# Fused attention and two MLPs on one core: the first weight's low halves and the early turned tiles formed by TensorE in PSUM, the second weight's norm from a Gram diagonal, and a new order

## The chip, the cores and the metric

One core of a Trainium2 chip. The metric is device microseconds of one execution; a stated time is the median of several runs. The engines are TensorE (PE, with its weight loads as PEld), VectorE (DVE), ScalarE (ACT), GpSimd (POOL) and SyncE (SP), which issues the DMAs.

## The reference

Three steps follow one another, on 2304 tokens:

```python
scores = scale * q @ k.T + alibi_bias          # 4 x 8 heads, 576 rows, D = 64, window of 128
x = softmax(scores) @ v                        # -> (2304, 512)
h = x @ w_in                                   # 512 x 1024
solu = h * softmax(h)
ln = (solu - mean) / sqrt(var + 1e-6) * g_ln
x = ln @ w_out                                 # 1024 x 512
h2 = x @ w2_in                                 # 512 x 2048
out = (h2 * sigmoid(h2)) @ w2_out              # 2048 x 512
```

q, k, v and the gain are float32. The four weights arrive as 64-bit floats, and the kernel turns them into 32-bit ones on the chip.

## The kernel before

The 2304 rows are 18 blocks of 128 (`i`), and 9 chunks of two blocks (`c`). Every product of the MLPs and of attention with V is made of float16 halves: a number is a high half plus a low half, and `high*high + high*low + low*high` are three float16 matmuls.

**Weights.** There are 48 pieces of 128x512 ("slots" 0 to 47 of the tile `W`): 8 of w_in, 8 of w_out, 16 of w2_in, 16 of w2_out. A piece is loaded into `stage` as pairs of 32-bit words (512 KB). `decode` makes float32 of it: ACT shifts the high words (L456), DVE scales the low words (L458) and puts both together (L460, result in `W`). From the decoded pieces a norm is taken, which gives a power of two as the weight's scale: as a rule by `gram`, a matmul of a tile with itself (L396), whose diagonal DVE sums (`trace`, L407) or takes the maximum of (`column_max`, L401). For w_out, ACT squares each piece with the gain as scale (L508) and a matmul with ones adds the squares up (L513). Then `split_weight` makes the halves. A table `E_W` says how for each slot: "G" scales the piece (L347 on ACT, L348 on DVE or L350 on POOL), copies it to float16 (L342 on ACT, L343 on DVE) and subtracts (L354 on DVE or L355 on POOL); "V" scales straight to the high half and makes the low half in one DVE instruction (L533).

**Blocks.** For each block `a_qk` makes scores in PSUM (`sa`, L688), `a_max` adds the bias and takes the row maximum on DVE (L714), and ACT takes exponentials (L719, tile `e`). `a_parts` splits the result into halves (tile `a`) and turns it by a DMA transpose on SP's queue (L746, tile `aT`). `a_av` multiplies with V (L773), `a_evac` scales (L786, `xm`), `x_turn` splits and turns again (`xT`). A table `ON_PE` has "D" for a DMA transpose, and "P" for a turn on TensorE: `turned_parts` transposes float32 128x128 tiles into PSUM (L566), ACT copies the high half out (L568), and DVE subtracts it from the PSUM tile (L569). "P" stands for `xT` of blocks 1 to 3 and for `lnT` of block 1. Then come the first product (`m1_in`, L820), the softmax gate and norm (`layer_norm`, L834 to L870), the turn to `lnT`, and for each chunk the second product (`m1_out`, L920), whose result is split into `y` (L925 on ACT, L928 on DVE). For each chunk `m2_in` (L957) makes eight tiles of h2, ACT and DVE form the gate (L966 to L970), and `m2_out` (L984) accumulates the result; ACT evacuates it (L990), SP stores it.

**Order.** All of this is recorded first. A list scheduler (`Sched`) then places the instructions, with hand-set costs and with priorities from the tables `RANK`, `SLOPE` and `LATER`; the emitted program is a fixed order on each engine. Engines run in that order and wait on semaphores. `PICK` fixes for each split which engine does it. `JOINT` says whether two head pairs of a block share one PSUM area, `ROOT` and `NORM` which engine makes the inverse root and the normalisation, `V_AT` at which block a batch's norm of V is placed. The PSUM tag `mm` has two buffers, which turned tiles, products and norms take in turn.

Of the kernel before, what the change touches and what calls it, by code (L numbers as in the profile page):

```python
# [298 lines left out]
def fused_kernel(ctx, tc, qk, qn, kn, vt, rel, w_in, w_out, g_ln, w2_in, w2_out, out):  # L299
# [89 lines left out]


# [82 lines left out]
    def load_weight(name, w, slot0, n, cols, gain=None, columns=False):
# [4 lines left out]
        for at in range(0, n, 2):  # L478
# [12 lines left out]
            def go(at, k, sl):  # L491
                if gain is None:
                    size = n // nf if columns else n
                    if at % size == 0:
                        sums[name] = Buf(ps_early, [P, 512], F32, "gram", 2)

                    def high(x):
                        w = W.tile.rearrange("p s c -> p (s c)").bitcast(BF16).rearrange("p (s c h) -> p s c h", h=2, c=512)
                        return w[:, sl, x * P:(x + 1) * P, 1]
                    gram(sums[name], 4, high, [(W, sl)], 4 * (at % size), 4 * size - 1, columns)  # L500
                    if at % size == size - 1:
                        if columns:
                            column_max(sums[name], acc, at // size)
                        else:
                            trace(sums[name], acc)
                    return
                sq = Buf(early, [P, 512], BF16, "sq", 2)
                act(512, lambda: A.activation(sq.tile, W[:, sl, :], AF.Square, scale=gain[:, k:k + 1]),  # L508
                    [(W, sl), gain], [sq], extra=1)
                if at == 0:  # L510
                    sums[name] = Buf(ps_early, [P, 512], F32, "gram", 2)
                c = sums[name]
                pe(216, lambda: T.matmul(c.tile, ones.tile, sq.tile, start=at == 0, stop=at == n - 1), [ones, sq], [c])  # L513
                if at == n - 1:
                    v(512, lambda: V.tensor_reduce(acc.tile, c.tile, AX.X, ALU.add), [c], [acc])
# [14 lines left out]

# [698 lines left out]
```

## Time and profile before

| | |
|---|---|
| time, median of 3 runs | 731.42 us (730.77 to 731.5) |
| profiled execution, its own time | 729.44 us |
| its span in the trace | 727.5 us |
| mean granted clock of TensorE | 0.981 |
| busy: PE, DVE, ACT, POOL | 93%, 61%, 48%, 19% of the span |

The span is the time from the first to the last instruction of the profiled execution; 1.94 us lie around it. The busy shares are means over the whole program, which has a first part in which weights are decoded and the first blocks run, and a long second part of matmuls.

### The profile page before, as it was taken

The page shows a single profiled execution, that of the slowest core. Times are in us where ns is not written, and L with a number is a line of the kernel's source. Part 1 is how long each engine was busy: PE and PEld are TensorE (multiplying, and loading weights), DVE is VectorE, ACT ScalarE, POOL GpSimd, SP SyncE. Part 2 cuts the span into 40 slices and gives each one's busy share as a digit, 9 for nine tenths or more (in the row PEclk, how much of TensorE's full clock was granted, in tenths as well). Part 3 has the DMA queues.
Part 4 walks back from the last instruction along what each step waited for, and adds up shares of the span by engine and source line. Part 5 has one row for each costly group of instructions (what it writes and reads, how often), then busy time and mean ns, then how long its engine had stood idle before and what let it go on. Part 6 is the DMA issues. An engine that isn't in the chain of part 4 may idle for free.

```text
span 727.5 us, 13956 instructions
## 1 busy us (share of the span) xinstructions
PE 674.3 (93%) x5541; PEld 464.0 (64%) x5541; DVE 444.8 (61%) x1125; ACT 346.2 (48%) x738; POOL 138.5 (19%) x140
## 2 busy tenths in 40 slices
PE   4563688999999999999999999999999999999997
PEld 2432367778565577667766676678566777657853
DVE  3899999996897747553556657547672523321220
ACT  5687668575646635444454445525341422231231
POOL 1223034322443312130322112101010200100000
PEclk9996799999999999999999999999999999999999
DMA  9999985593535534251723454334250421100000
GB/s 309 346 247 273 241 199 134 131 231 89 99 78 103 130 73 81 53 114 31 145 59 73 82 107 90 91 56 73 44 102 1 68 65 30 30 30 1 1 30 29
DMA packets 142209, 75.82 MB, mean 104 GB/s; under 512 B 126656, under 2 KB 126784, under 8 KB 142144
## 3 DMA queue, kind: packets, MB, share of 16 engines
q1 hardware_dynamic: 142144, 74.94, 44.2%
q8 instruction: 43, 0.70, 0.4%
q14 instruction: 22, 0.18, 0.1%
HBM read 39.52 MB, written 4.72 MB: 61 GB/s over the span
## 4 chain that ended last, share of the span: by engine, by line
PE 79%; DVE 14%; ACT 3%; issue 2%; DMA 1%; POOL 0%; DVEq 0%; POOLq 0%; ACTq 0%
PE mm L984 25%; PE mm L957 23%; PE mm L920 12%; PE mm L820 11%; PE sa L688 4%; DVE W L460 3%; PE mm L773 2%; DVE stage L458 2%; DVE e L714 1%; PE gram L396 1%; DVE W L533 1%; PE sa L773 1%; DVE W L354 1%; DMA aT<-a 1%; DVE W L348 1%
## 5 line engine op out<-in xcount | busy, mean ns | idle before, releaser
L957 PE MATMUL mm<-y,W 128*128 128x256 f16 x1728 | 210.4, 273 | 1.1 <-DVE t L967 0.7
L984 PE MATMUL mm<-W,g 128*128 128x512 f16 x864 | 204.9, 379 | 0.0
L957 PEld LDWEIGHTS <-W 128*128 128x128 f16 x1728 | 167.0, 98 | 39.8 <-issue 2.0
L984 PEld LDWEIGHTS <-g 128*128 128x128 f16 x864 | 81.8, 98 | 78.7 <-issue 0.2
L820 PE MATMUL mm<-W,xT 128*128 128x512 f16 x432 | 105.2, 390 | 1.7 <-DVE xT L569 1.0
L920 PE MATMUL mm<-lnT,W 128*128 128x256 f16 x864 | 104.8, 273 | 0.0
L920 PEld LDWEIGHTS <-W 128*128 128x128 f16 x864 | 84.0, 98 | 19.7 <-issue 0.5
L719 ACT ACTIVATE e<-e,mx 128x256 f32<-128x256 f32 (+1 forms) x144 | 70.0, 487 | 45.9 <-DVE mx L714 43.3
L970 DVE SCALAR_TENSOR_TENSOR g<-t,g 128x512 f16<-128x512 f32 x72 | 55.5, 774 | 53.7 <-ACT g L969 53.3
L355 POOL TENSOR_TENSOR a<-e,a 128x512 f16<-128x512 f32 (+1 forms) x45 | 54.9, 1222 | 143.2 <-ACT a L342 65.8
L969 ACT ACTIVATE g<-t 128x512 f16<-128x512 f32 x72 | 45.0, 626 | 72.6 <-PE mm L984 61.1
L967 DVE SCALAR_TENSOR_TENSOR t<-t,mm 128x512 f32<-128x512 f32 x72 | 48.7, 682 | 48.3 <-ACT t L966 48.3
L966 ACT ACTIVATE t<-mm,cs 128x512 f32<-128x512 f32 x72 | 48.1, 680 | 62.5 <-PE mm L957 58.6
L820 PEld LDWEIGHTS <-xT 128*128 128x128 f16 x432 | 42.7, 100 | 47.6 <-issue 4.6
L688 PE MATMUL sa<-k,q 64*128 64x128 f32 x544 | 49.4, 312 | 17.1 <-DVE mx L714 12.2
L714 DVE CUSTOM_DVE_ANT_0 e<-sa,table 128x256 f32<-128x256 f32 (+1 forms) x144 | 53.9, 400 | 11.3 <-PE sa L688 6.3
L688 PEld LDWEIGHTS sa<-k,q 64*128 64x128 f32 x544 | 38.5, 202 | 29.1 <-DVE mx L714 15.7
L928 DVE SCALAR_TENSOR_TENSOR y<-mm,cs,y 128x512 f16<-128x512 f32 x18 | 13.3, 748 | 57.1 <-ACT y L925 57.1
L834 DVE TENSOR_REDUCE lnst<-mm 128x1 f32<-128x1024 f32 x18 | 22.0, 1220 | 42.0 <-PE mm L820 42.0
L848 POOL TENSOR_SCALAR lnst<-lnst 128x1 f32<-128x1 f32 x17 | 3.5, 203 | 214.0 <-ACT mm L845 214.0
L925 ACT ACTIVATE y<-mm,cs 128x512 f16<-128x512 f32 x18 | 12.2, 686 | 64.0 <-PE mm L920 56.3
L773 PEld LDWEIGHTS <-aT 128*128 128x128 f16 x816 | 32.9, 101 | 15.2 <-issue 8.6
(151 smaller groups left out, 707.9 us busy)
## 6 DMA issues: line engine op xcount, KB each, us to landing
stage<-in_moe_w_in_dram SPq DMA_DIRECT2D x24, 512.0 KB, 5.3
stage<-in_moe_w_out_dram SPq DMA_DIRECT2D x24, 512.0 KB, 4.5
k<-in_kn_dram SPq DMA_DIRECT2D x18, 256.0 KB, 2.9
q<-in_qn_dram SPq DMA_DIRECT2D x18, 256.0 KB, 3.1
vraw<-in_vt_dram SPq DMA_DIRECT2D x18, 256.0 KB, 3.8
out_dram<-t SPq DMA_DIRECT2D x18, 256.0 KB, 2.3
aT<-a SPq DMA_TRANSPOSE x72, 3.3
lnT<-ln SPq DMA_TRANSPOSE x34, 3.2
```

Of the source, the lines that this page charges most:

```text
L355: ("G", cg(n), lambda: G.tensor_tensor(dst(), a(), b(), op), True)], r, w, pick=pick)
L688: T.matmul(SA[:, j, off + sl * P:off + (sl + 1) * P], q[rows, p, :], k[rows, p, :], start=True, stop=sl not in blank)
L714: v(n + 20, lambda j=j: V.tensor_tensor_reduce(e[:, j, lo:lo + n], SA[:, j, off + lo:off + lo + n], table[:, 2 * p + j, o:o + n], -0.125, ...
L719: act(n, lambda j=j: A.activation(e[:, j, lo:lo + n], e[:, j, lo:lo + n], AF.Exp, bias=mx[:, j:j + 1], scale=-1.0, accum_out=rs[:, 2 * p + ...
L773: T.matmul(heads(i)[:, h // 4, h % 4, :], t[:, (2 * ha + j) * nh + c, :], vb[sl][:, h, hv, :], start=(n == 0), stop=(n == 3 * nh - 1))
L820: T.matmul(pt[:, half * 512:(half + 1) * 512], x[:, hx, k, :], W16(2 * k + half, hw), start=(k == 0 and hx + hw == 0), stop=(k == KD - 1 a ...
L920: T.matmul(pt[:, ct % 2], W16(8 + k, hw)[:, ct * P:(ct + 1) * P], l[:, hx * KF1 + k, :], start=(k == 0 and hw + hx == 0), stop=(k == KF1 - ...
L957: T.matmul(pt[:, mm], W16(16 + 4 * k + m // 4, hw)[:, (m % 4) * P:(m % 4 + 1) * P], y[:, hx, k, :], start=(k == 0 and hw + hx == 0), stop= ...
L966: act(512, lambda: A.activation(t.tile, flat(pt.tile), AF.Tanh, scale=cs[:, 0:1]), [pt, (cs, 0)], [t], extra=1)
L967: v(512, lambda: V.scalar_tensor_tensor(out=t.tile, in0=t.tile, scalar=1.0, in1=flat(pt.tile), op0=ALU.add, op1=ALU.mult), [t, pt], [t])
L970: v(512, lambda: V.scalar_tensor_tensor(out=flat(g[:, 1]), in0=t.tile, scalar=2.0 ** -16, in1=flat(g[:, 0]), op0=ALU.mult, op1=ALU.subtrac ...
L984: T.matmul(pt.tile, g[:, hg, mm, b * P:(b + 1) * P], W16(32 + m, hw), start=(m == 0 and hg + hw == 0), stop=(m == KF2 - 1 and hg == 1))
```

## The change

Five things change.

1. `E_W` is "P" for the eight slots of w_in. The high half is scaled straight from the decoded piece (as in "V"). The low half is formed in PSUM: a float32 matmul of the piece with a diagonal matrix that holds the scale (`diag`), then a float16 matmul of the high half with minus the identity (`minus`), accumulated onto it; ACT or DVE copies the result out (DVE for slots 0 to 5, ACT for 6 and 7).
2. `ON_PE` has "Q" for `aT` and `xT` of blocks 0 to 3 and for `lnT` of blocks 0 and 1: turned on TensorE, high half copied out by ACT, minus the high half accumulated in PSUM, and the low half copied out by ACT too. The DMA transposes of these tiles go away, and so do the splits on DVE, ACT and POOL.
3. The norm of w_out comes from a Gram diagonal like the others, times the largest squared gain (`gain_max`, a handful of small instructions at the start). The eight squares on ACT and the eight ones-matmuls go away.
4. The last accumulation of the last block is done in two halves of columns, each with its own evacuation and store.
5. The tables of priorities, picks, `JOINT`, `ROOT`, `NORM` and `V_AT` are new, so the order changes on each engine.

```diff
+    minus = Buf(early2, [P, P], F16, "minus")
...
+    def low_part(pt, n, diag, whole, high, dst, r, w, pick):
+        def go():
+            if diag is not None:
+                T.matmul(pt[:, 0:n], diag.tile, whole(), start=True, stop=False)
+            T.matmul(pt[:, 0:n], minus.tile, high(), start=False, stop=True)
...
+        s.op([("A", 575, lambda: A.activation(dst(), pt[:, 0:n], AF.Copy), False),
+              ("V", cv(n), lambda: V.tensor_copy(dst(), pt[:, 0:n]), False)], [pt], w, pick=pick)
...
+    def diagonal(by):
+        d = Buf(early2, [P, P], F32, "diag", 2)
+        v(P, lambda: V.tensor_scalar(d.tile, unit.tile, by(), None, ALU.mult), [unit, by.src], [d], fast=True)
...
-                act(512, lambda: A.activation(sq.tile, W[:, sl, :], AF.Square, scale=gain[:, k:k + 1]),
-                    [(W, sl), gain], [sq], extra=1)
...
-                pe(216, lambda: T.matmul(c.tile, ones.tile, sq.tile, start=at == 0, stop=at == n - 1), [ones, sq], [c])
...
+                gram(sums[name], 4, high, [(W, sl)], 4 * (at % size), 4 * size - 1, columns)
...
+                if E_W[b] == "P":
...
+                    scaled(("wh", b), 512, lambda: W16(b, 0), lambda: W[:, a, :], scl, [(W, a), src], [(W, b)])
+                    pt = Buf(ps, [P, 512], F32, "mm", 2, free=True)
+                    low_part(pt, 512, diags[x], lambda: W[:, a, :], lambda: W16(b, 0), lambda: W16(b, 1),
+                             [(W, a), (W, b)], [(W, b)], ("we", b))
...
         act(n * P, lambda: A.activation(hi(), bank(), AF.Copy), [tp], [w[0]])
+        if low is not None:
+
+            def take():
+                T.matmul(bank(), minus.tile, hi(), start=False, stop=True, skip_group_check=True)
...
+            s.op([("A", 62 * n + 327, lambda: A.activation(lo(), bank(), AF.Copy), False),
+                  ("V", cv(n * P), lambda: V.tensor_copy(lo(), bank()), False)], [tp], [w[1]], pick=low)
+            return
...
+                halves = 2 if ends and mm and b and c == NB // 2 - 1 else 1
...
-    load_weight("wout", w_out, 8, 8, DM, gain=gcol)
+    load_weight("wout", w_out, 8, 8, DM, gain=gain_max())
...
-E_W = "GGGGGGVGGVVGVVGGVGGVVGGVGVGGGGGVGVVGGGGVGVVGGGGG"
+E_W = "PPPPPPPPGVVGVVGGVGGVVGGVGVGGGGGVGVGGGGGVGVVGGGGG"
...
-JOINT = ".......JJJJJJJJJJJ"
-ROOT = "GGGGGGGGGGGGGGVGGG"
-NORM = "VAAAGAAAGGAVVAVGGV"
-ON_PE = {"a": "DDDDDDDDDDDDDDDDDD", "x": "DPPPDDDDDDDDDDDDDD", "l": "DPDDDDDDDDDDDDDDDD"}
...
+JOINT = "......JJJJSJJJSJJJ"
+ROOT = "GGGGVVGGGGGGGVVVGG"
+NORM = "VAAAGGGAGGAVGAVGGV"
+ON_PE = {"a": "QQQQDDDDDDDDDDDDDD", "x": "QQQQDDDDDDDDDDDDDD", "l": "QQDDDDDDDDDDDDDDDD"}
...
-V_AT = [0, 1, 9, 10]
+V_AT = [0, 2, 9, 9]
```

The order on DVE where the pieces of w_in are split, while pieces of w_out are decoded between (`W<-stage` puts a decoded piece together). Before:

```order
L354 TENSOR_TENSOR W<-W 128x512
L460 SCALAR_TENSOR_TENSOR W<-stage 128x512
L458 TENSOR_SCALAR stage<-stage 128x512
L354 TENSOR_TENSOR W<-W 128x512
L460 SCALAR_TENSOR_TENSOR W<-stage 128x512
L348 TENSOR_SCALAR W<-W,swin 128x512
L458 TENSOR_SCALAR stage<-stage 128x512
L354 TENSOR_TENSOR W<-W 128x512
L460 SCALAR_TENSOR_TENSOR W<-stage 128x512
L354 TENSOR_TENSOR W<-W 128x512
L533 SCALAR_TENSOR_TENSOR W<-W,swin 128x512
```

And of the change, in the same place (`W<-mm` takes a low half out of PSUM):

```order
L348 TENSOR_SCALAR W<-W,swin 128x512
L401 CAST W<-mm 128x512
L480 SCALAR_TENSOR_TENSOR W<-stage 128x512
L478 TENSOR_SCALAR stage<-stage 128x512
L401 CAST W<-mm 128x512
L480 SCALAR_TENSOR_TENSOR W<-stage 128x512
L478 TENSOR_SCALAR stage<-stage 128x512
L401 CAST W<-mm 128x512
L480 SCALAR_TENSOR_TENSOR W<-stage 128x512
L478 TENSOR_SCALAR stage<-stage 128x512
L348 TENSOR_SCALAR W<-W,swin 128x512
```

The subtractions from `W` have become copies from PSUM; the scalings write the high half.

The order on PE in the first product of block 0 (`mm_74` is its PSUM tile). Before, a ones-matmul of w_out's norm stands between its matmuls:

```order
L820 MATMUL mm_74<-W,xT 128x512
L513 LDWEIGHTS ones
L513 MATMUL gram<-sq,ones 128x512
L820 LDWEIGHTS xT
L820 MATMUL mm_74<-W,xT 128x512
```

Of the change, a Gram matmul of w_out and the two matmuls of a low half of w_in:

```order
L413 LDWEIGHTS W
L413 MATMUL gram<-W 128x128
L397 MATMUL mm<-W,diag 128x512
L398 LDWEIGHTS minus
L398 MATMUL mm<-W,minus 128x512
L877 LDWEIGHTS xT
L877 MATMUL mm_74<-W,xT 128x512
```

In PE's order the low halves are now made between the matmuls that use them.

The order on POOL after its first memsets (`a` is the split of the exponentials, `x` that of `xm`, `W<-W` a low half of a weight). Before:

```order
L355 TENSOR_TENSOR a_138<-e,a_138 128x256
L355 TENSOR_TENSOR a_359<-e,a_359 128x256
L350 TENSOR_SCALAR W<-W,swin 128x512
L355 TENSOR_TENSOR a_463<-e,a_463 128x512
L355 TENSOR_TENSOR a_482<-e,a_482 128x512
L355 TENSOR_TENSOR x_133<-xm,x_133 128x512
L355 TENSOR_TENSOR W<-W 128x512
L355 TENSOR_TENSOR a_546<-e,a_546 128x512
L355 TENSOR_TENSOR a_570<-e,a_570 128x512
L350 TENSOR_SCALAR W<-W,gs 128x512
L355 TENSOR_TENSOR a_704<-e,a_704 128x512
L355 TENSOR_TENSOR W<-W 128x512
```

Of the change:

```order
L584 TENSOR_SCALAR minus<-unit 128x128
L350 TENSOR_SCALAR W<-W,gs 128x512
L355 TENSOR_TENSOR W<-W 128x512
L905 TENSOR_SCALAR lnst<-lnst 128x1
L907 TENSOR_TENSOR lnst<-lnst,half 128x1
L355 TENSOR_TENSOR W<-W 128x512
L905 TENSOR_SCALAR lnst<-lnst 128x1
L907 TENSOR_TENSOR lnst<-lnst,half 128x1
L350 TENSOR_SCALAR W<-W,sw2in 128x512 x6
L355 TENSOR_TENSOR W<-W 128x512 x3
```

The splits of the first blocks' `a` and `x` have left POOL's queue; six scalings of w2_in have come in.

## Rows read from the trace of the kernel before

**Rows 1.** Page, section 1: engine, busy us (share of the span), instructions.

```profile
PE 674.3 (93%) x5541; PEld 464.0 (64%) x5541; DVE 444.8 (61%) x1125; ACT 346.2 (48%) x738; POOL 138.5 (19%) x140
```

**Rows 2.** Windows over the span: busy time of each engine, PE's granted clock, DMA share.

```profile
0.00:16.00 16.00, 6.94 (x45) 5.04 (x45) 4.39 (x29) 9.18 (x27) 2.42 (x15) 1.00 0.91 312
16.00:124.60 108.60, 71.21 (x617) 48.07 (x618) 103.80 (x276) 78.66 (x163) 29.11 (x29) 0.89 0.91 245
124.60:157.10 32.50, 30.31 (x273) 23.00 (x272) 31.78 (x64) 21.81 (x43) 11.72 (x10) 0.95 0.66 167
157.10:240.00 82.90, 82.70 (x723) 56.38 (x724) 68.94 (x171) 49.30 (x114) 29.23 (x26) 1.00 0.49 100
240.00:727.50 487.50, 483.14 (x3884) 331.51 (x3882) 235.88 (x591) 187.23 (x393) 66.05 (x61) 1.00 0.31 63
```

**Rows 3.** Timeline of PE, 100 to 200 us: start, length, line, idle before.

```profile
124.62 1.26 PE L957 MATMUL mm<-y,W 128*128 128x256 f16 x6 [0.18 <-DVE y L928]
...
183.95 5.34 PE L820 MATMUL mm<-W,xT 128*128 128x512 f16 x24
```

**Rows 4.** Waits of DVE, 16 to 124.6 us: total, times, longest.

```profile
DVE e L714 <- PE sa L688: 1.6, 2, 1.3
DVE e L714 <- PE sa L773: 1.2, 2, 0.9
```

**Rows 5.** DVE by line and form, 0 to 124.6 us: count, busy, mean ns.

```profile
L460 DVE SCALAR_TENSOR_TENSOR W<-stage 128x512 uint32<-128x512 uint32 x37 | 27.6, 754 | 0.9 <-ACT stage L456 0.4
L458 DVE TENSOR_SCALAR stage<-stage 128x512 uint32<-128x512 uint32 x39 | 19.2, 500 | 0.0
...
L354 DVE TENSOR_TENSOR W<-W 128x512 f16<-128x512 f32 x8 | 6.8, 851 | 0.0
...
L533 DVE SCALAR_TENSOR_TENSOR W<-W,sw2in 128x512 f16<-128x512 f32 x3 | 2.1, 739 | 0.0
L354 DVE TENSOR_TENSOR a<-e,a 128x512 f16<-128x512 f32 x3 | 2.0, 682 | 0.2 <-ACT a L342 0.2
...
L343 DVE CAST W<-W 128x512 f16<-128x512 f32 x5 | 2.0, 409 | 0.0
...
L569 DVE TENSOR_TENSOR xT<-mm,xT 128x512 f16<-128x512 f32 x2 | 1.4, 678 | 0.0
```

**Rows 6.** Timeline of DVE, single instructions.

```profile
43.16 0.47 DVE L348 TENSOR_SCALAR W<-W,swin 128x512 f32<-128x512 f32 x1
43.56 0.41 DVE L458 TENSOR_SCALAR stage<-stage 128x512 uint32<-128x512 uint32 x1
...
71.58 1.62 DVE L460 SCALAR_TENSOR_TENSOR W<-stage 128x512 uint32<-128x512 uint32 x1
```

**Rows 7.** Timeline of POOL, around 71 us.

```profile
71.50 1.15 POOL L355 TENSOR_TENSOR a<-e,a 128x512 f16<-128x512 f32 x1
```

**Rows 8.** Timeline of PE, pieces of the first 100 us.

```profile
24.57 1.23 PE L688 MATMUL sa<-k,q 64*128 64x128 f32 x8
...
51.65 0.71 PE L688 MATMUL sa<-k,q 64*128 64x128 f32 x8
...
73.86 1.11 PE L566 MATMUL mm<-unit,xm 128*128 128x128 f32 x4 [0.92 <-DVE xm L786]
...
94.92 1.10 PE L566 MATMUL mm<-unit,e 128*128 128x128 f32 x8 [0.17 <-ACT e L863]
...
97.89 1.09 PE L396 MATMUL gram<-W 128*128 128x128 bf16 x16 [0.21 <-DVE accw2in L401]
...
99.08 0.66 PE L566 MATMUL mm<-unit,xm 128*128 128x128 f32 x4
99.77 0.49 PE L688 MATMUL sa<-k,q 64*128 64x128 f32 x4
```

**Rows 9.** ACT by line and form, 0 to 157 us: count, busy, mean ns.

```profile
L568 ACT ACTIVATE xT<-mm 128x512 f16<-128x512 f32 x3 | 1.8, 593 | 1.2 <-PE mm L566 1.2
```

**Rows 10.** Timeline of ACT, the end.

```profile
723.73 0.69 ACT L990 ACTIVATE t<-mm,cs 128x512 f32<-128x512 f32 x1 [0.55 <-PE mm L984]
```

More of the change, by code (lines that the diff above doesn't have):

```diff
@@ L408, in trace, with norm_scale @@
           [c, unit], [junk, acc])
-    def norm_scale(name, parts, whole=False, columns=False):
+    def norm_scale(name, parts, gain=None, columns=False):
         al, u, r = (Buf(const, [P, 1], F32, "nrm" + x, 2) for x in "bcd")
+        whole = Buf(early2, [P, 1], F32, "nrmw", 1) if gain is not None else None
         big, scl = Buf(const, [P, 1], F32, "Q" + name), Buf(const, [P, 1], F32, "s" + name)
@@ L469, in decode, with gain_max @@
                                               op0=ALU.logical_shift_right, op1=ALU.bitwise_or), [st] + w, w)
+    def gain_max():
+        s.at("gain", 0)
+        sq, top, most = (Buf(early2, [P, n], F32, "gain" + x) for x, n in (("s", KF1), ("t", 1), ("m", 1)))
+        v(50, lambda: V.tensor_tensor_reduce(sq.tile, gcol.tile, gcol.tile, 1.0, 0.0, ALU.mult, ALU.max, top.tile),
+          [gcol], [sq, top])
+        pt = Buf(ps, [P, 512], F32, "mm", 2, free=True)
+        pe(240, lambda: T.matmul(pt[:, 0:P], top.tile.to_broadcast([P, P]), unit.tile, start=True, stop=True),
+           [top, unit], [pt])
+        v(P, lambda: V.tensor_reduce(most.tile, pt[:, 0:P], AX.X, ALU.max), [pt], [most])
+        return most
     scales, sums = {}, {}
@@ L491, in go @@
             def go(at, k, sl):
[L492 to L506, printed above, removed]
@@ L507, in go @@
[L507 to L515 removed]
+                size = n // nf if columns else n
@@ L565, in go @@
             for x in range(n):
-                T.transpose(bank()[:, x], src(x), unit.tile)
+                T.matmul(bank()[:, x], src(x), unit.tile, is_transpose=True, start=x == 0 or low is None,
+                         stop=True, skip_group_check=low is not None)
         pe(210 * n, go, r + [unit], [tp])
         act(n * P, lambda: A.activation(hi(), bank(), AF.Copy), [tp], [w[0]])
+        if low is not None:
+            def take():
+                T.matmul(bank(), minus.tile, hi(), start=False, stop=True, skip_group_check=True)
+            pe(n * P / 2.37, take, [w[0], minus], [tp])
+            s.op([("A", 62 * n + 327, lambda: A.activation(lo(), bank(), AF.Copy), False),
+                  ("V", cv(n * P), lambda: V.tensor_copy(lo(), bank()), False)], [tp], [w[1]], pick=low)
+            return
         v(n * P, lambda: V.tensor_tensor(lo(), bank(), hi(), ALU.subtract), [tp, w[0]], [w[1]])
@@ L794, in x_turn @@
         s.at("evac", i, 1)
[L795 removed]
+        if ON_PE["x"][i] in "PQ":
             s.at("xturn", i)
@@ new lines @@
+SLOPE = {"aturn": 35.81, "av": -22.15, "evac": 5.41, "exp": 9.83, "gain": 16.7, "gate": -24.75, "in": 31.01,
+         "in2": -10.84, "load": 3.76, "lparts": 23.06, "max": -32.36, "max1": -15.42, "norm": -8.42, "out": 17.83,
+         "out2": 27.63, "parts": -17.07, "qk": 27.54, "s0": 17.4, "s16": 6.12, "s32": 15.93, "s8": 26.64,
+         "share": 10.04, "store": -46.18, "table": 16.92, "tav": -15.44, "tevac": 3.76, "texp": 20.57, "tpar": 9.55,
+         "tscore": 8.82, "tsub": 19.12, "vload": 1.27, "vnorm": 8.8, "vsplit": 14.4, "w0": -5.4, "w16": -0.78,
+         "w32": -1.01, "w8": -15.67, "xturn": 33.55, "y": -39.86}
```

205 lines of the change are left out of this document (122 added, 83 removed), and 42 rows, old and new, of the table LATER.

## The prediction

> **What bounds the kernel now.** PE is busy for 93% of the span, DVE for 61% [rows 1]. These are means over two parts with different limits, so the windows come next [rows 2]. From 157.1 us on PE does not stop: 82.70 of 82.90 us, then 483.14 of 487.50, whose gap is mostly the end. Before that it is DVE that is full: 103.80 of 108.60 us between 16 and 124.6, 31.78 of 32.50 between 124.6 and 157.1. PE has 71.21 of the 108.60, ACT 78.66, POOL 29.11. In 0 to 16 us nobody is full: data is on its way.
>
> The mark between the parts is the first matmul of `m2_in`, at 124.62 us, released by DVE's `y` [rows 3]. I counted what stands behind that mark in PE's order, in both kernels: 1728 matmuls of L957, 864 of L984 (of the change, six of them of half the width in place of three), 360 of L820, 768 of L920, 648 with V, 208 score matmuls in both. Only Gram matmuls differ, 44 and 36. So the rest of the program is the same work on a full engine, and the end moves with the time at which this mark is reached, as long as PE is then fed. The question is what the change does to the first 124.6 us, which DVE sets: its named waits between 16 and 124.6 us are small, 1.6 and 1.2 us on PE [rows 4]; with the rest it is 4.8 us of idle time [rows 2].
>
> **The change on DVE before the mark.** DVE's order has 293 instructions before the first `y` in the kernel before and 295 in the change, so nothing is to be seen from the number; the kinds differ. Durations are undisturbed ones: 0.68 us for a 512-wide instruction with two inputs and for one that reads PSUM (`a` of L354, and L569) [rows 5], 0.74 for a low half made in one (L533) [rows 5], 0.41 for a 512-wide copy (L343) [rows 5], 0.47 for a scaling and 0.41 for L458 [rows 6].
>
> Gone before the mark: 6 subtractions of weights and 3 of `a` (9 x 0.68 = 6.1), 2 of `a` of half the width (0.8), 4 subtractions from turned tiles (2.7), 5 copies of `a` and W and 1 of `x` (6 x 0.41 = 2.5), 2 half-wide copies and 1 of `ln` (1.2), 2 low halves in one (1.5), one `vs` (0.7), one `xm` (0.7), the sum of w_out's squares (0.7). Together 16.9 us.
> New before the mark: 9 more scalings (they leave ACT: 9 x 0.47 = 4.2), 6 copies of low halves from PSUM, which no row shows; they lie between a copy from SBUF, 0.41, and L569, 0.68, and as they read PSUM I take 0.68: 4.1 (bound below 2.5). Three more L460 and one more L458 (2.4: decoding that was done later before), one pair of L714 (0.5), `diag`, the trace and small instructions of the new norm (1.9). Together 13.1 us. Net: **-3.8 us** (-5.4 by the lower bound).
>
> **POOL's part.** DVE's means are above the undisturbed values: L460 754 ns over 37, L458 500 over 39, L354 on W 851 over 8 [rows 5]. Single rows show why: an L460 that starts at 71.58 takes 1.62 us [rows 6], while POOL runs a 1.15 us subtraction from 71.50 [rows 7]. Over the first 124.6 us these three lines alone have 37 x 0.07 + 39 x 0.09 + 8 x 0.17 = 7.5 us above undisturbed; with the casts and scalings I put it at 9. POOL was busy for 29.1 us meanwhile. In the change the splits of `a` and `x` of the first blocks have left its queue: before the mark I count 6 weight subtractions (6 x 1.15), 6 scalings of w2_in and 1 with the gain (an estimate of 0.8 each, the middle between DVE's 0.47 and POOL's 1.15), `minus` and three roots, some 15 us. Half the cause, half the effect: **-4.5 us**; bounds 0 and -9.
>
> **ACT and PE before the mark.** ACT's order has 121 instructions before the first `y`, then 136. Evacuations of turned tiles cost 593 ns [rows 9], and it loses squares, casts and scalings for them; 15 more at that price are 9 us at most, 88 of some 100. It does not become the bound. PE gets, at the rate of its later part: 8 float32 matmuls with `diag`; four more score rows take 0.49 -> 0.72 us for two float32 matmuls of 128 columns side by side (at 99.77 and at 51.65) [rows 8], so 0.23 for 128 columns, 0.92 for 512, 7.4 together. 28 matmuls with `minus` of 512 columns at 5.34/24 = 0.22 [rows 3], 6.2, and four of 256, 0.4. 68 more float32 transposes: eight took 1.10, four 0.66 [rows 8], so 0.11 each, 7.5. 40 more Gram matmuls at 1.09/16 [rows 8], 2.7; less eight ones-matmuls, 1.8. Sum **+22.4 us** on 71.2, in a stage of about 100. It fits, if not by much, and hides under DVE; without that cover it costs what the slower rival below says.
>
> The wait in DVE's order that the change adds: its second instruction now needs the gain, a load issued after two blocks' k and q; the block's first maximum stands behind it, and ACT and PE behind that. DVE is idle for 11.6 of the first 16 us [rows 2], so I cost it at nothing; uncovered it is a microsecond or two.
>
> PE and ACT now pass each turned tile back and forth (transpose, copy, `minus`, copy) in fixed order, with the decoding in between. Some of that will show as new idle time on DVE: nothing below, the whole gain above. I take 2 us, less than half of the 4.8 it has now.
>
> **Behind the mark.** Eight Gram matmuls fewer: -0.6. The last evacuation, 0.69 us for 512 columns [rows 10], is of half the width: -0.2; its store I leave as it is. The end runs on: -0.8.
>
> **Sum.** -3.8 - 4.5 + 2.0 - 0.8 = -7.1 us. The profiled execution's span of 727.5 becomes 720.4, its own 729.44 becomes 722.3; the median of the runs lies 2.0 above that execution, so 731.42 becomes **724.3 us**. A measurement of this kernel tells about 0.2%, 1.5 us, from no change.
>
> **The rivals.**
> *More than that.* POOL's disturbance goes wholly (-9), copies from PSUM are cheap (-5.4), and no idle time is added: 731.4 - 15.2 = 716. For it: the early subtractions on POOL are those that hit the decoding. Against it: the six scalings are new there, just before the mark.
>
> *No gain: given back behind the mark.* Between 157.1 and 240 us DVE is busy for 68.94 of 82.90 us [rows 2] and PE only just gets its operands. If PE arrives 7 us early, DVE must bring the splits of w2_out and the blocks' work forward, of which the change takes less away there; or DVE's idle time in the first stage grows by the whole gain because it waits for PE and ACT in turn. Either way 731, between 728.5 and 733. For it: the exchange of DVE work before the mark is a mere 3.8 us. Against it: DVE still has 14 us of slack in those 83.
>
> *Slower: PE becomes the bound of the first stage.* [...] The granted clock is 0.89 between 16 and 124.6 us as a mean [rows 2], but eight score matmuls took 1.23 us at 24.57 and 0.71 at 51.65; four transposes took 1.11 at 73.86 and 0.66 at 99.08 [rows 8]: a factor of 1.7, the lower level for much of the stage. If all the additions run on it, they are 22.4 x 1.7 = 38 us: 71.2 + 38 = 109 us of work in a stage that had 108.6, of which 37.4 were PE waiting. If 10 us of waits remain, the mark comes at 16 + 109 + 10 = 135, 10.5 late: 731.4 + 10.5 - 0.8 = 741. It decides from the point where work and waits on PE pass 108.6: at the high level with more than 15 us of waits, at the low one with none. Against it: more work in the same time gives PE fewer pauses, and the score row at 51.65 shows the higher level already in the midst of the stage.
> [...]
>
> **How the numbers follow.** The forecast, mark reached 4 to 12 us earlier: 0.55 (718 to 728). More than that: 0.19. Given back: 0.14. PE as the bound: 0.12. The range is from 716.5 to 731.5: it holds the forecast, most of the case above it in gain and of the one without. Faster by over 0.2% (below 729.9): the first two and a little of the third, 0.76. Within 0.2%: 0.12. Slower: 0.12.
>
> **What would show it.** The first L1014 at about 117.5 us; DVE still at 95% between 16 us and there; POOL at about half of its 29 us; L480's mean near 700 ns; PE at 90 us or more before the mark, and without pauses behind it. If the mark comes early and the end does not, the gain was given back, and PE shows idle time between 150 and 240 us. If DVE falls below 90% in the first stage and waits for PE or ACT, the chain through PSUM is the bound. If PE's Gram and transpose rows keep their doubled lengths up to 100 us, the clock is.

## The result and the profile after

The changed kernel takes **722.52 us** (median of 4 runs, 722.11 to 722.8), beside 731.17 us for the kernel before on the same chip (4 runs): a ratio of 0.9881, 95% interval 0.9864 to 0.9899. Run again later beside other kernels, it took 721.63 against 732.62: 0.9853, 0.9835 to 0.9871. It is faster, by 1.2 to 1.5%. The profiled execution took 722.11 us, its span is 720.3.

The page's busy line of the kernel after, to be held against [rows 1]:

```profile
PE 689.9 (96%) x5687; PEld 473.5 (66%) x5687; DVE 432.4 (60%) x1156; ACT 348.0 (48%) x748; POOL 125.0 (17%) x122
```

PE has 15.6 us more work in a span that is 7.2 us shorter. Where the time went is seen when the span is cut at the same place of the program as in [rows 2], the first matmul of `m2_in`, and then at the same distances behind it; busy time of each engine, then PE's granted clock and the DMA share:

```profile
0.00:16.00 16.00, 5.69 (x35) 4.00 (x35) 3.93 (x24) 8.24 (x20) 2.06 (x15) 1.00 0.90 305
16.00:118.47 102.47, 88.25 (x778) 59.04 (x779) 95.66 (x283) 83.38 (x184) 19.40 (x20) 0.97 0.70 230
118.47:150.97 32.50, 31.75 (x300) 24.83 (x299) 29.65 (x73) 21.06 (x42) 11.40 (x8) 0.95 0.61 160
150.97:233.87 82.90, 82.10 (x695) 54.90 (x693) 67.71 (x172) 46.35 (x105) 27.25 (x22) 1.00 0.46 93
233.87:720.30 486.43, 482.11 (x3885) 330.68 (x3883) 235.42 (x608) 189.00 (x398) 64.88 (x58) 1.00 0.30 62
```

That matmul in the timeline of PE; in the kernel before it stands at 124.62 [rows 3]:

```profile
118.47 2.29 PE L1014 MATMUL mm<-y,W 128*128 128x256 f16 x12
```

So 6.15 us of the 7.2 are won ahead of this mark and 1.05 behind it (602.88 us before, 601.83 now). Up to the mark DVE is busy for 3.93 + 95.66 = 99.59 us, where it had 108.19, and idle for 18.88, where it had 16.41. VectorE's waits from 16 us to the mark are small and spread (total, times, longest); before, waits for two kinds of TensorE's results, scores and products with V, made up most of what had a name [rows 4]:

```profile
DVE W L480 <- ACT stage L476: 1.9, 3, 1.2
DVE e L770 <- PE mm L598: 0.8, 1, 0.8
DVE xm L843 <- PE sa L830: 0.7, 1, 0.7
DVE lnst L919 <- POOL lnst L907: 0.7, 1, 0.7
```

VectorE by line and form up to the mark; L480 and L478 answer to L460 and L458 of [rows 5], L401 is the new copy out of PSUM:

```profile
L480 DVE SCALAR_TENSOR_TENSOR W<-stage 128x512 uint32<-128x512 uint32 x40 | 27.0, 685 | 2.0 <-ACT stage L476 1.9
L478 DVE TENSOR_SCALAR stage<-stage 128x512 uint32<-128x512 uint32 x40 | 17.7, 447 | 0.6 <-DMA stage<-in_moe_w_out_dram 0.6
...
L401 DVE CAST W<-mm 128x512 f16<-128x512 f32 x6 | 4.1, 680 | 0.2 <-PE mm L398 0.2
...
L354 DVE TENSOR_TENSOR W<-W 128x512 f16<-128x512 f32 x2 | 2.2, 1092 | 0.0
```

The two decoding steps have come down from 754 and 500 ns to 685 and 447. On TensorE the timeline shows what the stage consists of now: scores, turned tiles, and the two matmuls of a low half (L397, in float32, stands as two matmuls a tile in the trace, 16 for the eight tiles).

```profile
16.44 1.05 PE L598 MATMUL mm<-unit,e 128*128 128x128 f32 x4
...
19.93 1.23 PE L744 MATMUL sa<-k,q 64*128 64x128 f32 x8
...
23.39 0.73 PE L744 MATMUL sa<-k,q 64*128 64x128 f32 x8
...
26.42 0.60 PE L598 MATMUL mm<-unit,e 128*128 128x128 f32 x4
...
37.37 0.72 PE L744 MATMUL sa<-k,q 64*128 64x128 f32 x8
...
44.11 1.07 PE L397 MATMUL mm<-W,diag 128*128 128x512 f32 x2
45.02 0.38 PE L398 MATMUL mm<-W,minus 128*128 128x512 f16 x1
```

The same eight score matmuls take 1.23 us at 19.93 and 0.73 at 23.39, and four transposes 1.05 at 16.44 and 0.60 at 26.42. "Lower level" and "upper level" stand for these two paces of TensorE, a factor of 1.7 apart in these rows. The upper one is there from about 23 us, though the granted clock reads 1.00 on either side (19 to 21 us, 21 to 24 and 24 to 28). In the kernel before, eight score matmuls still took 1.23 us at 24.57 [rows 8].

### The profile page after: what moved, and what is told of

The parts are those of the page before. It is cut to its first block, busy times and chain, and to the rows that moved or that the text cites. A ratio compares the mean times of both kernels' runs of the same rounds, so it can differ in the third digit from the quotient of the medians.

```text
span 720.3 us, 14231 instructions
## 1 busy us (share of the span) xinstructions
PE 689.9 (96%) x5687; PEld 473.5 (66%) x5687; DVE 432.4 (60%) x1156; ACT 348.0 (48%) x748; POOL 125.0 (17%) x122
## 4 chain that ended last, share of the span: by engine, by line
PE 81%; DVE 9%; DMA 3%; ACT 3%; issue 2%; SPq 1%; POOL 0%; ACTq 0%; DVEq 0%
PE mm L1046 24%; PE mm L1014 24%; PE mm L877 12%; PE mm L977 12%; PE sa L744 5%; DVE W L480 2%; PE mm L830 2%; DMA aT<-a 1%; DMA q<-in_qn_dram 1%; DVE stage L478 1%; PE sa L830 1%; DVE e L770 1%; DMA stage<-in_moe_w_out_dram 1%; PE gram L413 1%; PE mm L397 1%
## 5 line engine op out<-in xcount | busy, mean ns | idle before, releaser
L1014 PE MATMUL mm<-y,W 128*128 128x256 f16 x1728 | 208.1, 273 | 0.8 <-DVE t L1024 0.6
L877 PE MATMUL mm<-W,xT 128*128 128x512 f16 x432 | 99.9, 384 | 0.2 <-ACT mm L902 0.2
L1027 DVE SCALAR_TENSOR_TENSOR g<-t,g 128x512 f16<-128x512 f32 x72 | 52.8, 737 | 51.6 <-ACT g L1026 51.2
L744 PE MATMUL sa<-k,q 64*128 64x128 f32 x544 | 47.6, 303 | 9.0 <-DMA q<-in_qn_dram 7.6
L893 ACT ACTIVATE e<-mm,lnst,sig 128x1024 f32<-128x1024 f32 x18 | 21.7, 1206 | 65.6 <-DVE lnst L892 60.1
L744 PEld LDWEIGHTS sa<-k,q 64*128 64x128 f32 x544 | 36.8, 194 | 23.8 <-DMA k<-in_kn_dram 7.6
L355 POOL TENSOR_TENSOR a<-e,a 128x512 f16<-128x512 f32 (+1 forms) x26 | 32.8, 1264 | 78.6 <-ACT a L342 33.2
L355 POOL TENSOR_TENSOR ln<-e,ln 128x1024 f16<-128x1024 f32 x11 | 24.2, 2201 | 97.2 <-ACT ln L342 76.4
```

The costliest lines, as they stand in the source:

```text
L355: ("G", cg(n), lambda: G.tensor_tensor(dst(), a(), b(), op), True)], r, w, pick=pick)
L744: T.matmul(SA[:, j, off + sl * P:off + (sl + 1) * P], q[rows, p, :], k[rows, p, :], start=True, stop=sl not in blank)
L877: T.matmul(pt[:, half * 512:(half + 1) * 512], x[:, hx, k, :], W16(2 * k + half, hw), start=(k == 0 and hx + hw == 0), stop=(k == KD - 1 a ...
L1014: T.matmul(pt[:, mm], W16(16 + 4 * k + m // 4, hw)[:, (m % 4) * P:(m % 4 + 1) * P], y[:, hx, k, :], start=(k == 0 and hw + hx == 0), stop= ...
L1027: v(512, lambda: V.scalar_tensor_tensor(out=flat(g[:, 1]), in0=t.tile, scalar=2.0 ** -16, in1=flat(g[:, 0]), op0=ALU.mult, op1=ALU.subtrac ...
```

## The experiments

A time is compared by its ratio to the kernel before, run beside it; the changed kernel stands at 0.9881 and 0.9853. "The mark" is the first matmul of `m2_in` throughout.

**Order alone.** The kernel before with the new tables of priorities and picks, `JOINT`, `ROOT`, `NORM` and `V_AT`; the forms stay. Two small parts of the change belong to the forms here: slot 34 of `E_W`, a piece of w2_out, is "G" instead of "V", and some of the scheduler's hand-set costs are higher (VectorE's two decoding steps 580 and 575 instead of 512 and 530). This kernel has those of the kernel before.

```diff
 E_W = "GGGGGGVGGVVGVVGG..."
 ON_PE = {"a": "DDDDDDDDDDDDDDDDDD", "x": "DPPPDDDDDDDDDDDDDD", "l": "DPDDDDDDDDDDDDDDDD"}
-RANK, SLOPE, LATER, PICK, JOINT, ROOT, NORM, V_AT of the kernel before
+RANK, SLOPE, LATER, PICK, JOINT, ROOT, NORM, V_AT of the change
```

> The forms of the kernel before (w_in split, turns by DMA, norm by squares, one store at the end), in an order made from the changed tables. My theory (the gain is DVE work and GpSimd's disturbance of DVE, taken away ahead of the first m2_in matmul): the order alone takes none of it away; counted by the undisturbed durations, DVE has 118.7 us ahead of its first y, against 114.1 in the kernel before and 110.3 in the changed one. So about 736 us, between 730 and 741. Rival (the new order is what gains): 722 to 726.

Measured: 742.71 us, ratio 1.0154 (1.0132 to 1.0176). The order saves nothing without the forms; it costs more than the 741 that was the upper end of the expectation. The windows of this kernel, cut at its mark of 131.46:

```profile
16.00:131.46 115.46, 77.16 (x638) 52.51 (x638) 109.72 (x284) 73.72 (x150) 34.90 (x34) 0.84 0.88 242
131.46:740.40 608.94, 596.05 (x4860) 408.18 (x4858) 337.76 (x858) 255.89 (x547) 100.00 (x87) 1.00 0.34 70
```

VectorE is 95% busy from 16 us to the mark, much as in the kernel before (96%), but with 109.72 us of work instead of 103.80: the new order puts more in front of the mark, which the new forms would have made room for. The stretch behind the mark takes 6 us more than before, 608.94 instead of 602.88, with the same 596 us of TensorE's work in it; the rest is idle time of TensorE.

**Forms alone.** The changed kernel with the tables of before, except for the entries that the new forms need.

```diff
-RANK, SLOPE, LATER, PICK, JOINT, ROOT, NORM, V_AT of the change
+RANK, SLOPE, LATER, PICK, JOINT, ROOT, NORM, V_AT of the kernel before
 E_W = "PPPPPPPP..."
 ON_PE = {"a": "QQQQDDDDDDDDDDDDDD", "x": "QQQQDDDDDDDDDDDDDD", "l": "QQDDDDDDDDDDDDDDDD"}
```

> The changed kernel's code and forms, in an order made from the tables of the kernel before. My theory: DVE has 110.6 us ahead of the first y, 3.5 less than the kernel before, and GpSimd's early splits are gone; so most of the gain is there even in an order made for something else: 723 to 728. Rival (order): 730 or more. Second rival (the chain through PSUM needs an order of its own, DVE then waits for ScalarE and TensorE): over 733.

Measured: 731.66 us, ratio 0.9991 (0.9979 to 1.0004). No gain, against expectation. Its windows up to its mark of 121.73 and behind it, and VectorE's largest waits before it:

```profile
16.00:121.73 105.73, 88.79 (x764) 59.88 (x763) 94.58 (x278) 90.53 (x196) 16.77 (x16) 0.96 0.68 229
121.73:730.00 608.27, 600.69 (x4889) 413.33 (x4887) 327.26 (x813) 259.07 (x547) 104.26 (x95) 0.99 0.33 70
```

```profile
DVE e L770 <- PE sa L830: 2.2, 2, 1.7
DVE lnst L891 <- PE mm L877: 2.2, 1, 2.2
DVE e L770 <- PE sa L744: 1.7, 1, 1.7
```

VectorE's relief is all there: 3.85 us in the first 16, 94.58 up to the mark, 98.4 together, 9.8 less than before. But the mark comes only 2.9 us earlier: the rest has become idle time, and the largest waits in it are for TensorE. And the stretch behind the mark is 5.4 us longer than before, with 600.69 us of TensorE in it where there were 596.2 (674.3 less 6.94 and 71.21, [rows 1, 2]). Little of this is work left over: seven matmuls of turned tiles, 2.0 us, against twelve Gram matmuls fewer, 0.7 us. Just ahead of the mark TensorE waits 3.6 us for VectorE's `y`, and its granted clock is then 0.50 for eight microseconds, where the kernel before had 0.57 for four. Behind the mark, this kernel and then the kernel before:

```profile
121.73:126.00 4.27, 3.58 (x22) 2.34 (x21) 4.27 (x5) 2.46 (x4) 3.86 (x3) 0.50 0.17 38
126.00:130.00 4.00, 4.00 (x28) 3.01 (x26) 3.80 (x8) 1.44 (x3) 0.00 (x0) 0.50 0.45 146
```

```profile
124.62:128.62 4.00, 3.75 (x26) 2.43 (x26) 4.00 (x5) 1.40 (x3) 1.70 (x2) 0.57 0.54 100
128.62:132.62 4.00, 4.00 (x20) 1.85 (x19) 4.00 (x9) 3.03 (x8) 2.50 (x2) 1.00 0.41 76
```

The time is as the rival by order had it, 730 or more. What the forms free on VectorE has to be collected by an order in which VectorE and TensorE do not wait for each other.

**One form undone at a time.** First w_in's low halves as before (POOL and VectorE subtract), then all tiles turned as before, each with the new tables.

```diff
-E_W = "PPPPPPPPGVVGVVGG..."
+E_W = "GGGGGGVGGVVGVVGG..."
```

> The changed kernel with the low halves of w_in made as before (scale, copy, subtract), all else as changed. My theory: DVE has 115.8 us ahead of the first y, 5.5 more, and GpSimd gets some subtractions back (1 to 2 us more on DVE); TensorE has 9 us less and that is worth nothing. So +6 to +8: 728 to 731. Rival (TensorE is near its bound in the first stage): 722 or less.

Measured: 735.96 us, ratio 1.0054 (1.0033 to 1.0075), the mark at 124.53 with 25.31 us of POOL in front of it.

```diff
-ON_PE = {"a": "QQQQDDDDDDDDDDDDDD", "x": "QQQQDDDDDDDDDDDDDD", "l": "QQDDDDDDDDDDDDDDDD"}
+ON_PE = {"a": "DDDDDDDDDDDDDDDDDD", "x": "DPPPDDDDDDDDDDDDDD", "l": "DPDDDDDDDDDDDDDDDD"}
```

> The changed kernel with the early tiles turned as before (DMA transposes, three xT and one lnT on TensorE with the low half by DVE). My theory: DVE has 127.5 us ahead of the first y, 17 more than the changed kernel, and GpSimd has the early splits again: +15 to +22, 737 to 745. Rival (what the turned tiles gain is the latency of the DMA transposes, not DVE work): 726 to 731, about the time of the kernel before.

Measured: 752.85 us, ratio 1.0281 (1.0255 to 1.0307), the mark at 143.79 with 34.49 us of POOL. Both come out above their theory and their rival. By the ratios they are 12.7 and 29.3 us slower than the changed kernel, together several times the gain of the whole change. VectorE's work up to the mark accounts for 7.4 and 21.0 us of that (106.98 and 120.57 us in all, instead of 99.59); the stretch behind the mark is 7.6 and 6.2 us longer than in the changed kernel, and in the second kernel TensorE's weight loads wait 7.9 us for tiles from DMA transposes, which was the rival's point. So these are not prices of the parts: that the tables place work which the undone form no longer makes room for is the likely reason, but it is not shown by itself. The next kernels therefore leave the order of all other instructions as the change has it and only add or exchange instructions in place.

**Work added to one engine.** Four kernels, each the changed kernel with some 5 to 25 us of work put on one engine in the first stage.

```diff
+                for _ in range(2 if 8 <= j < 16 else 1):      # VectorE: w_out's last decoding step twice
                     V.scalar_tensor_tensor(out=out(), in0=high(), scalar=3, in1=low(), ...)
...
+            for _ in range(5 if pick[0] == "we" else 0):      # GpSimd: 40 subtractions of 128 columns
+                G.tensor_tensor(spare.tile, unit.tile, high()[:, 0:P], ALU.subtract)
...
+                for x in range(3):                            # TensorE: the product with diag three times
+                    T.matmul(pt[:, 0:n], diag.tile, whole(), start=True, stop=x < 2)
...
+                for _ in range(3 if 8 <= j < 16 else 0):      # ScalarE: 24 copies of 128 columns
+                    A.activation(spare.tile, unit.tile, AF.Copy)
```

> The changed kernel with eight of VectorE's last decoding steps of w_out's tiles (tiles 8 to 15) done twice; the order of everything else is as in the changed kernel. Eight more at 0.685 us are 5.5 us of VectorE. Theory (VectorE sets the length of the stretch up to the first m2_in matmul in the changed kernel too): 4 to 6 us longer, and the first m2_in matmul later by as much. Rival (the order, the loads or TensorE set it now, and VectorE has slack): 0 to 2 us.

> The changed kernel with 40 subtractions of 128 columns more on GpSimd (some 0.4 us each, 16 us in all) in the stretch from about 38 to 56 us, in which it has nothing to do and nobody waits for it; all other engines keep their order. Theory (work on GpSimd slows VectorE's instructions that run beside it, by about 0.3 us for each us, as the difference of the means of the same decoding steps between the two kernels suggests): VectorE's means in that stretch rise, and the time by 3 to 5 us. Rival (the shorter means in the changed kernel come from elsewhere): no longer instructions there, 0 to 0.5 us.

> The changed kernel with the float32 product with the diagonal run three times for each of w_in's 8 tiles: 16 more products, some 0.95 us each, 15 us more of TensorE between 38 and 55 us, in the same order. Theory (TensorE has slack there, the new products are hidden): 0 to 4 us longer, VectorE waits a little more for them. Rival (TensorE, 86% busy in that stage, is the next bound at once): 8 to 15 us.

> The changed kernel with 24 copies of 128 columns more on ScalarE (some 0.23 us each, 5.5 us in all), three behind each shift of w_out's tiles 8 to 15; all other engines keep their order. Theory (ScalarE has slack): 0 to 2 us longer. Rival (the low parts that ScalarE now also handles have made it the bound, or its results come last): 4 to 6 us.

Measured: VectorE 727.48 us, ratio 0.9936 (0.9915 to 0.9957), mark at 124.19, 5.7 later. GpSimd 726.18, 0.9923 (0.9908 to 0.9939), mark at 123.49, 5.0 later. TensorE 737.66, 1.0081 (1.0066 to 1.0096), mark at 132.32, 13.9 later. ScalarE 726.28, 0.993 (0.9909 to 0.9952), mark at 122.17, 3.7 later. By the ratios, against 0.9881 and 0.9853, these are 4.0 to 6.1, 3.1 to 5.1, 14.6 to 16.7 and 3.6 to 5.6 us.

What the delay consists of is seen on VectorE up to the mark of each kernel:

| kernel | busy, us | idle, us |
|---|---|---|
| the change | 99.59 | 18.88 |
| work added to VectorE | 104.78 | 19.41 |
| work added to GpSimd | 103.99 | 19.50 |
| work added to TensorE | 100.19 | 32.13 |
| work added to ScalarE | 99.65 | 22.52 |

The first two additions lengthen VectorE's work, the last two its waits.

*GpSimd's part is as the theory had it.* It ran the added instructions from 38.16 to 63.82 us. VectorE in just that stretch, first in the changed kernel:

```profile
L480 DVE SCALAR_TENSOR_TENSOR W<-stage 128x512 uint32<-128x512 uint32 x14 | 9.5, 681 | 0.0
L478 DVE TENSOR_SCALAR stage<-stage 128x512 uint32<-128x512 uint32 x15 | 6.4, 424 | 0.0
L401 DVE CAST W<-mm 128x512 f16<-128x512 f32 x6 | 4.1, 680 | 0.2 <-PE mm L398 0.2
L770 DVE CUSTOM_DVE_ANT_0 e<-sa,table 128x256 f32<-128x256 f32 x6 | 2.4, 414 | 0.0
L348 DVE TENSOR_SCALAR W<-W,swin 128x512 f16<-128x512 f32 x3 | 1.4, 482 | 0.4 <-PE mm L397 0.4
...
L698 DVE SCALAR_TENSOR_TENSOR vs<-vraw,sv,vs 128x512 f16<-128x512 f32 x1 | 0.7, 745 | 0.0
```

and with GpSimd at work:

```profile
L485 DVE SCALAR_TENSOR_TENSOR W<-stage 128x512 uint32<-128x512 uint32 x12 | 9.6, 808 | 0.0
L483 DVE TENSOR_SCALAR stage<-stage 128x512 uint32<-128x512 uint32 x13 | 7.5, 575 | 0.0
L406 DVE CAST W<-mm 128x512 f16<-128x512 f32 x6 | 4.1, 678 | 0.0
L348 DVE TENSOR_SCALAR W<-W,swin 128x512 f16<-128x512 f32 x3 | 1.9, 648 | 0.0
L775 DVE CUSTOM_DVE_ANT_0 e<-sa,table 128x256 f32<-128x256 f32 x4 | 1.6, 408 | 0.0
...
L703 DVE SCALAR_TENSOR_TENSOR vs<-vraw,sv,vs 128x512 f16<-128x512 f32 x1 | 0.9, 910 | 0.0
```

Instructions that take all their large operands from SBUF are 0.13 to 0.17 us longer (681 to 808, 424 to 575, 482 to 648, 745 to 910); those that read a tile from PSUM keep their time (680 and 678, 414 and 408). So the low halves' new copies out of PSUM kept their time beside this work of GpSimd, and 22.6 us of it cost VectorE 4.4 us. No wait on GpSimd in that stretch explains the delay: VectorE's only named wait for it up to the mark is 0.7 us, as in the changed kernel. That emptying GpSimd's queue gained as much as filling it costs is an inference; for TensorE the kernels further down show that the two directions can differ.

*TensorE's part is not: the rival holds.* TensorE's rows in the stretch of w_in's low halves, changed kernel and then the one with tripled products:

```profile
38.00:56.00 18.00, 17.98 (x113) 9.51 (x112) 17.41 (x46) 12.59 (x25) 0.00 (x0) 1.00 0.84 286
56.00:70.00 14.00, 9.86 (x111) 6.85 (x110) 14.00 (x40) 13.43 (x30) 2.71 (x2) 0.92 0.94 329
```

```profile
38.00:56.00 18.00, 18.00 (x68) 8.17 (x67) 9.36 (x22) 7.25 (x16) 0.00 (x0) 1.00 0.57 188
56.00:70.00 14.00, 13.98 (x80) 7.47 (x79) 9.24 (x27) 5.44 (x11) 0.00 (x0) 1.00 0.57 180
```

In the changed kernel TensorE is busy for 17.98 of 18 us there, and VectorE for 17.41: both are full. The mean of 86% over the whole stage hid it. The added products are 13.7 us of TensorE (22.3 instead of 8.6 up to 80 us), the mark comes 13.9 us later, and VectorE falls to 9.36 of 18 and 9.24 of 14 us.

*VectorE and ScalarE.* The VectorE kernel came out as its theory had it, ScalarE's above its theory (0 to 2 us) and at or near the rival (4 to 6). In both a second effect runs along. Windows of the changed kernel, then of the one with more VectorE work:

```profile
32.00:36.00 4.00, 3.11 (x41) 2.56 (x42) 3.41 (x13) 3.87 (x11) 0.00 (x0) 1.00 0.80 227
36.00:40.00 4.00, 3.66 (x39) 2.25 (x37) 4.00 (x22) 3.38 (x9) 0.00 (x0) 1.00 0.96 349
```

```profile
32.00:36.00 4.00, 2.66 (x29) 1.92 (x29) 3.90 (x10) 4.00 (x12) 0.00 (x0) 0.74 0.73 259
36.00:40.00 4.00, 4.00 (x34) 3.42 (x34) 3.96 (x21) 1.90 (x6) 0.00 (x0) 0.50 0.97 311
```

The added work delays TensorE's operands, TensorE pauses (2.66 of 4 us busy instead of 3.11), and its granted clock falls to 0.50 just ahead of the stretch in which it is full. Little of it reaches the mark: of the 5.7 us, 5.2 are VectorE's work and 0.5 its idle time. In ScalarE's kernel it is otherwise: VectorE's work is unchanged and its idle time 3.6 us longer, TensorE is busy for 1.79 us of 4 from 32 to 36 us, and the granted clock is 0.72 and 0.85 in the eight microseconds behind. How much of the 3.7 us is ScalarE's work and how much the lower level isn't settled by these runs.

**TensorE relieved.** Work added to TensorE shows in full; the question was whether work taken from it also pays. In two kernels low halves of w_in are made without TensorE and without GpSimd, by one VectorE instruction from SBUF; with them the changed kernel itself was run again.

```diff
-    pe(..., go, r + [minus] + ..., [pt])          # both matmuls
-    V.tensor_copy(dst(), pt[:, 0:n])              # tiles 0 to 5
+    V.scalar_tensor_tensor(out=dst(), in0=whole(), scalar=scales["win"][1].tile, in1=high(),
+                           op0=ALU.mult, op1=ALU.subtract)   # tiles 0 to 5, or 0 to 3
+    A.activation(dst(), pt[:, 0:n], AF.Copy)      # second kernel: tiles 4 and 5, after both matmuls
```

> The changed kernel once more, unaltered, as the measure for the two kernels beside it on the same chip: 722 to 723 us.

> The changed kernel, with six of w_in's eight low halves (those that VectorE took out of PSUM by a copy of 0.68 us) formed by one VectorE instruction from SBUF (tile times scale less high half, 0.74 us for that form elsewhere in the trace), and TensorE's two products for each left out, 6 x 1.34 = 8 us of TensorE between 38 and 54 us; GpSimd stays out, and all else keeps its order. Theory (VectorE, 97% busy in that stretch, is level with TensorE there, so that TensorE's relief is worth little): between 0.5 us longer and 1 us shorter than the changed kernel. Rival (the runs with tripled products read the other way round: TensorE alone bounds that stretch): 4 to 8 us shorter.

> As the kernel with VectorE's one-instruction form, but for four of the eight low halves only; the other four stay in PSUM and ScalarE takes all of them out, where the changed kernel gives it two. VectorE has 4 x 0.74 instead of 6 x 0.68 us, 1.1 us less, TensorE 5.4 us less, ScalarE two copies more, 1.3 us. Theory (VectorE sets the length): 0.5 to 1.5 us shorter than the changed kernel. Rival (ScalarE, on which 5.5 us of copies cost 3.7 us, gives it back): no change to 1 us longer.

Measured: 721.63 us again (0.9853, 0.9835 to 0.9871), 720.65 with six (0.9845, 0.9822 to 0.9867), 721.08 with four (0.9842, 0.9822 to 0.9862). The three can't be told apart at the 1.5 us or so that the intervals allow, and their marks lie at 117.96, 118.64 and 117.84. The windows of the kernel with six:

```profile
38.00:56.00 18.00, 13.03 (x103) 6.60 (x99) 17.75 (x45) 12.89 (x26) 0.00 (x0) 1.00 0.83 282
56.00:70.00 14.00, 9.06 (x104) 6.25 (x103) 14.00 (x42) 13.75 (x30) 2.71 (x2) 0.95 0.96 348
```

TensorE is busy for 5 us less in 38 to 56 us, and nothing is won: VectorE is full at 17.75. Its copy out of PSUM took 680 ns, the one instruction that replaces it 741. For six of w_in's eight low halves, then, the way through PSUM is worth nothing measurable over a VectorE instruction that leaves GpSimd alone. That what counts in this part of the change is GpSimd's absence follows from this only together with the kernel of added subtractions; no run here puts w_in's subtractions back on GpSimd with the order kept.

**The norm undone, the order kept.**

```diff
-                gram(sums[name], 4, high, [(W, sl)], 4 * (at % size), 4 * size - 1, columns)
+                A.activation(sq.tile, W[:, sl, :], AF.Square, scale=2.0 ** -3.5)
+                T.matmul(c.tile, ones.tile, sq.tile, start=at == 0, stop=at == n - 1)
```

> The changed kernel with one of its parts undone: the sum of w_out's squares is formed by eight squares on ScalarE (0.71 us each, 5.7 us) and eight products with ones (0.22 us each) again, where the Gram matmuls (8 x 0.39 us) stood; VectorE sums 512 columns at the end instead of 128 (0.4 us more); all else keeps its order. Theory (ScalarE's place in the order counts, as its extra copies showed, 0.67 us for each us): 3 to 5 us longer than the changed kernel. Rival (this part of the change is worth nothing, ScalarE is 81% busy in the stage): 0 to 1 us.

Measured: 728.99 us, ratio 0.9962 (0.9948 to 0.9976), the mark at 125.27, 6.8 later. The rival, worth nothing, is out, but the theory's 3 to 5 us are too little. As much as the whole change won at the mark, 6.15, is lost with this one part, so prices of parts taken in this way don't add up to the gain. The same windows of this kernel show part of why:

```profile
32.00:36.00 4.00, 2.16 (x23) 1.59 (x24) 3.02 (x11) 4.00 (x12) 0.00 (x0) 0.86 0.86 272
36.00:40.00 4.00, 3.02 (x14) 1.78 (x13) 2.44 (x16) 2.11 (x6) 0.00 (x0) 0.50 0.91 344
40.00:44.00 4.00, 3.79 (x24) 2.52 (x24) 2.14 (x9) 2.64 (x6) 0.00 (x0) 0.50 0.13 50
```

ScalarE is full from 32 to 36 us (4.00), TensorE is busy for only 2.16 of these 4 us and is granted 0.50 for the eight microseconds that follow; between 30 and 70 us it waits 3.5 us for squares. Eight score matmuls take 1.23 us at 37.24, where the changed kernel needed 0.72 at 37.37. Up to the mark VectorE is busy for 100.59 us and idle for 24.68, 5.8 more than in the changed kernel. So the squares cost waits first and TensorE's lower level after them; the shares of the two are not separated.

The turned tiles have no such kernel: what they are worth with the order kept stays open.

## Why the prediction was right, step by step

The forecast was 724.3 us and a span of 720.4; measured were 722.52 and 720.3. The mechanism, less work on VectorE ahead of the mark, holds under the new order. The span was met to 0.1 us, the time to 1.8: the 2.0 us that were put between the profiled execution and the median were 0.4 (722.11 and 722.52).

- **VectorE ahead of the mark**, -3.8 by exchange and -4.5 by GpSimd's absence: -8.3 forecast, 108.19 to 99.59 = -8.6 measured. GpSimd's share by the same reckoning as for [rows 5]: L480 40 x 0.005, L478 40 x 0.037, L354 2 x 0.41, some 2.5 us above undisturbed where it was 7.5, so -5.0, which leaves -3.6 for the exchange. That GpSimd slows VectorE was an inference from coincident rows; the kernel with 40 added subtractions shows it.
- **GpSimd "at about half of its 29 us"** was wrong: 19.40 from 16 us to the mark. Half the cause was the reasoning, two thirds of it stayed, and yet two thirds of the effect went, so that -4.5 came near -5.0 by luck. What remains lies late: 14.16 of the 19.40 us fall between 90 us and the mark, where only 5 of the 40 last decoding steps (L480) stand. When GpSimd works counted here more than for how long.
- **The copy out of PSUM**, taken at 0.68 with a lower bound of 0.41: 680 ns.
- **New idle time on VectorE**, +2.0: from 4.80 to 6.81 us between 16 us and the mark, +2.0, and from 16.41 to 18.88 with the first 16 us, +2.5. The 2 us were taken from no row, so the size is partly luck. The wait for the gain, costed at nothing, is there (4.52 us until 7.93) and hidden: the first decoding starts at 14.76, in the kernel before at 15.38. VectorE's share of 95% from 16 us to the mark came out at 93%.
- **Behind the mark**, -0.8: -1.05. "Given back behind the mark" did not happen here; in the kernel with the old order the stretch behind the mark took 5.4 us more than before, so the rival was a real one, and the new order averts it.
- **ScalarE**, said not to become the bound, 88 us of some 100: up to the mark it is busy for 91.62 of 118.47. That mean hid what windows show: it is full from 40 to 44 us and from 56 to 68. The sum gave the new norm of w_out 0.7 us of VectorE and nothing for the eight squares that leave ScalarE; putting the squares back in place cost 6.8 us at the mark. The sum has no term for this, and why it came out all the same isn't shown.
- **TensorE**, +22.4 us: up to the mark 78.15 to 93.94, +15.8. The added instructions are as counted, but what was there before runs shorter (a first-product matmul 442 ns before and 394 now, a score matmul 384 and 342). It has the upper level from about 23 us on, but for the stretch from 68 to 76 us, where the granted clock is 0.50 and then 0.67. The granted clock between 16 us and the mark is 0.97, where it was 0.89.
- **The slower rival**, additions at the lower level: it fell because the level rose, eight score matmuls from 1.23 us at 19.93 to 0.73 at 23.39, where the kernel before still had 1.23 at 26.68. Turned tiles, scores and Gram matmuls stand close together there, and no run separates what raised it. But "It fits, if not by much" was too kind to TensorE: from 38 to 56 us it has no room at all.

What the prediction didn't see is that the gain belongs to forms and order together. It costed the forms by counting them in the new order, which is why the sum came out. Counted in the old one VectorE has nearly the same work ahead of `y` (110.6 us against 110.3 in the expectations above), so it would have forecast the same and been wrong by the whole gain.

## What to carry to other kernels

Where two engines are full side by side, more work on one of them can show in full and less work on it bring nothing, as with TensorE here (13.7 us more cost 13.9, 5 us less won nothing); look for such stretches in windows, since a stage's mean of 86% can hold one of 100%. Keep GpSimd's work out of a full stretch in which VectorE works from SBUF (22.6 us of it cost VectorE 4.4 us here), and put it where VectorE has slack or reads PSUM (680 ns for a copy without it, 678 beside it). A form that frees an engine pays only under an order that uses what it frees: here the forms alone and the order alone both won nothing. So price forms with the order fixed, by adding or exchanging instructions in place.

## What the hardware showed that was not expected

- GpSimd's work stretched some VectorE instructions and not others: 0.13 to 0.17 us for those fed from SBUF, nothing for those that read a tile from PSUM (680 and 678, 414 and 408 ns). GpSimd itself needed 565 ns for 128 columns.
- A pause on TensorE can be followed by a lower granted clock: in the kernel with squares, after 2.16 of 4 us busy, it was 0.50 for eight microseconds, and eight score matmuls took 1.23 us instead of 0.72. That a wait ahead of a full stretch can cost more than itself is inferred from this; the shares are not separated. A lower clock does not always follow: in the kernel with six low halves made by VectorE, TensorE is busy for only 13.03 of 18 us from 38 to 56 us, and the granted clock of that stretch is 1.00.
- The lower level isn't always seen in the granted clock: at 19.93 us eight score matmuls took 1.23 us while it read 1.00, and 0.73 at 23.39. Durations of a known instruction are the safer sign. What raised the level there stays open.
